# Expert slots: VectorE and ScalarE in written order, with the weight splits dealt out by a sequencer

## The chip, the cores and the metric

One Trainium2 chip, one core of it. The metric is the device time of one execution in microseconds (us), the median of three timed runs. One further execution was profiled; its trace is what is read here.

## What is computed

Causal attention (2 batches, 12 heads, 448 tokens, head size 64), then a dense layer with a squared rectifier, then a mixture of 8 experts in which every token goes to one expert:

```python
x = attention(q, k, v)                                # 896 tokens x 768
h = np.maximum(x @ w_in, 0.0); x = h * h @ w_out      # 768 -> 2048 -> 768
xn = x / (norm(x) + 1e-6); en = emb / (norm(emb) + 1e-6)
idx = argmax(xn @ en.T / tau); gate = softmax(xn @ en.T / tau)[idx]
for e in range(8):
    h = np.maximum(x[idx == e] @ w1[e], 0.0)          # 768 -> 1024
    out[idx == e] = gate * (h @ w2[e])                # 1024 -> 768
```

## The kernel before, in words

All products run in fp32r, each operand split into a high and a low part, and three products (high-high, high-low, low-high) are summed in PSUM. The first 377 us are attention, the dense layer (`phase_a`, `b_tiles`) and the routing of the first tiles; they are not touched. What follows is a row of expert slots, each with one expert's weights and a fixed number of tokens:

- **Slot E** (form D, 256 tokens of the expert that is fullest after five of seven tiles) starts at 377 us. While it runs, the generator `first()` finishes the routing of the last tile (`route_tile`: logits, norm, one-hot `OH`, ranks) and then the tables of all other slots (`tables`, then `table` with the product `tabp`, L600). It advances a step at each "hook": `ft0` lists the column blocks of the first product (`mm1_w`, eight blocks `ft`), `ft1` and `ft2` the row blocks of the second (`mm2`, eight blocks `fc`) for its two halves of 128 tokens. The hooks are built as a dictionary with the block's number as key. After the table come the gathers of the next slot's tokens (`slot_x`, L831, an indirect DMA from `ydram` issued by POOL) and their transposes `xt` on PE (L841).
- **Slots M0, T2, M1, T3, L0, T4** follow (the first is the rest of slot E's expert, the numbers are the table's). M has 160 tokens (128 and 32), T has 64, L has 384 (a D pass of 256 and an S pass of 128).

Each slot's weights are 16 tiles of 128x768. Eight DMAs by SP bring two tiles each into one of six raw buffers; ScalarE copies a tile into its high part `mh` (L59), VectorE subtracts it into the low part `ml` (L66). A tile takes the place of the same tile of the slot before, so it can be split only when PE has read that one for the last time, and the raw buffer comes free only when both its tiles are split.

The products are evicted by the same two engines. In M (`mm1_w`) ScalarE copies one half of the PSUM tile to `hsum` (L710), VectorE adds the other half (L711), ScalarE rectifies each part (L715) and VectorE forms the low parts (L716). In T and S (`mm1_x`) the same pair leaves `hr` (L777, L778), PE transposes it (`turn`, L751), and rectifier and low part follow (L753, L754). All these PSUM tiles, and the `xt` and `yt` ones, come from one pool, `ps_h`, of three buffers. Results leave as `osb` (L814 to L817).

PE's order is written by hand (`manual_schedule`). The order of VectorE and ScalarE is found by a list scheduler, which ranks ready instructions by its own estimates and so spreads the table work and the weight splits wherever an engine looks free.

Of the kernel before, what the change touches and what calls it, by code (L numbers as in the profile page):

```python
# [13 lines left out]
ALU = mybir.AluOpType  # L14
# [6 lines left out]
P = 128  # L21
# [11 lines left out]
def f32(ap):  # L33
    return ap.bitcast(F32)
# [5 lines left out]
    turn2=[1, 3], ft0=[0, 1, 2, 3, 4], ft1=[3], ft2=[2, 4, 5, 6], ew=[2, 4, 10, 10, 10, 12, 14], stop=0, mlo="V", xh="A", h2="A",  # L40
# [4 lines left out]
    vh="AG", kl="G", vl="G", pth="AAAA", nrm="GGGGGGG", u0=1, order=[2, 1, 3, 0, 4])  # L45


def build(tc, qkd, vd, w_in, w_out, emb, tau, wm, cst, out, dbg_y=None):
# [618 lines left out]
    def pieces(s, res):  # L667

        for i2 in range(8):
            if i2 == 0 or (i2 == CFG["first"] and s[4] is not None):  # L670
                ereg = nc.sync.value_load((s[3] if i2 == 0 else s[4])[0:1, :], min_val=0, max_val=E - 1)
            r = state["raw"] % (NXR + 2)
            state["raw"] += 1
            if r < NXR:
                raw = mo["xraw"][:, r]
            else:
                raw = spool.tile([P, 2 * DM], F32, tag="raw", name="mraw")
            DMA.dma_start(out=raw, in_=wm[bass.ds(ereg, 1), :, 2 * i2:2 * i2 + 2, :].rearrange("o p a c -> (o p) (a c)"))
# [9 lines left out]
            yield  # L688
# [5 lines left out]
    def mm1_w(s, w, hooks):  # L694
# [3 lines left out]
        for ft in range(8):  # L698
            step(hooks, ft)
            ps = ps_h.tile([P, 512], F32, tag="h", name="hps")  # L700
            if s[0] == "M":
# [26 lines left out]
            V.scalar_tensor_tensor(out=lo, in0=x, scalar=0.0, in1=f32(hi), op0=ALU.max, op1=ALU.subtract)  # L728

# [13 lines left out]
    def mm1_x(s, w, hooks):  # L743
# [13 lines left out]
        for q in range(4):  # L757
# [21 lines left out]
            hrs.append(hr)  # L779

# [91 lines left out]
    def mm1(s, w, hooks):  # L872
        return (mm1_w if s[0] in "DM" else mm1_x)(s, w, hooks)
# [37 lines left out]
    def tables():  # L911
# [18 lines left out]
        z = z.rearrange("p e k -> p (e k)")  # L930
        key = small([NZ], "key")
# [5 lines left out]
        V.reduce_sum(out=zr, in_=gt, axis=AX.X)  # L937
        zc = small([NZ, len(STEPS)], "zc")
# [12 lines left out]
        V.tensor_tensor(out=zo, in0=zo, in1=over, op=ALU.mult)  # L951
        zp = small([E, NK], "zp")
# [18 lines left out]

        k3 = small([NTI, NK], "k3")
# [14 lines left out]
        V.tensor_tensor(out=k3[:, :, 0:NK - 1], in0=k3[:, :, 0:NK - 1], in1=k3[:, :, 1:], op=ALU.subtract)  # L987
        tokw = bpool.tile([P, NTI, E, NK], BF16, tag="ysb", bufs=2, name="tokw")
# [30 lines left out]
    def run_slot(ps, w, feeds, at_end=False):  # L1019
# [8 lines left out]
        if len(ps) == 2:  # L1028
# [5 lines left out]
            more = mm1(ps[1], w, {})  # L1034
            it = feeds()
            if CFG["joint"]:
                next(it, None)
                mm2([(s, 1), (ps[1], 0)], w, hooks_for(CFG["xfj"], it, more))
            else:
                mm2([(s, 1)], w, more or {})  # L1040
                next(it, None)
                mm2([(ps[1], 0)], w, hooks_for(CFG["xfd"], it))
# [5 lines left out]
        parts = [(s, i) for i in range(len(FORM[s[0]]))]
        if len(parts) == 2 and not CFG["joint"]:
            mm2(parts[:1], w, hooks_for(CFG["xfd"], it, more))  # L1050
            all_of(it)
            mm2(parts[1:], w, {})
        else:
            mm2(parts, w, hooks_for(CFG["xfd"], it, more), split=at_end)
            all_of(it)
# [10 lines left out]

    it = first()
# [6 lines left out]
    all_of(it)  # L1074
    for i, ps in enumerate(slots_now):
        w = ew
        if i:
            w, it = slot_w(ps[0])
            all_of(it)
# [100 lines left out]
```

## Time and profile before

| | us |
|---|---|
| three timed runs | 584.53, 585.80, 588.54 (median 585.8) |
| profiled execution | 583.95 |
| its span, first to last instruction | 582.2 |
| PE busy in the span | 558.6 (96%) |
| VectorE (DVE) busy | 399.6 (69%) |
| ScalarE (ACT) busy | 291.5 (50%) |

An engine's busy time is the time in which at least one of its instructions is under way. PE's matmuls overlap one another, so PE counts as busy also where they follow at half pace. "Granted clock" is the share of TensorE's full clock of 2.4 GHz; 0.5 is the lower of its two levels, 1.2 GHz.

### The profile page before, as it was taken

How to read it: one execution, taken by the hardware profiler on the slowest of the kernel's cores; microseconds unless marked ns; L12 is line 12 of the kernel's file. 1: busy time of each engine (PE TensorE's matmuls, PEld its weight loads, DVE VectorE, ACT ScalarE, POOL GpSimd, SP SyncE). 2: the span in 40 equal slices, each digit the busy share in tenths (PEclk: the TensorE clock that was granted, in tenths of full speed). 3: DMA queues.
4: the chain of work that ended last, by engine and by line, in shares of the span. 5: the costliest groups of instructions: out<-in, count | busy, mean ns of one | idle time of the engine just before them, and what ended most of it. 6: DMA issues, size and time to landing. Idle time of an engine off the chain costs nothing.

```text
span 582.2 us, 9781 instructions
## 1 busy us (share of the span) xinstructions
PE 558.6 (96%) x3501; PEld 512.2 (88%) x3501; DVE 399.6 (69%) x901; ACT 291.5 (50%) x654; POOL 188.3 (32%) x204
## 2 busy tenths in 40 slices
PE   6999999999999999999999999899998999899994
PEld 3888788889999999999999999799997888799993
DVE  6878688955777878597664376975387986932641
ACT  4768678523343433434333226721478877923651
POOL 7676667854445544221000001001203412500010
PEclk8899999999999999999999999999999999899998
DMA  7757542223444655351000009404887987950310
GB/s 222 176 145 230 125 100 70 84 81 110 156 148 142 204 177 184 130 179 70 23 28 28 1 28 377 164 3 149 306 254 239 339 329 237 337 176 29 110 49 5
DMA packets 28233, 86.51 MB, mean 149 GB/s; under 512 B 2822, under 2 KB 13062, under 8 KB 28176
## 3 DMA queue, kind: packets, MB, share of 16 engines
q1 hardware_dynamic: 26640, 79.51, 42.3%
q0 software_dynamic: 1536, 6.29, 2.9%
q8 instruction: 29, 0.48, 0.3%
q14 instruction: 28, 0.23, 0.1%
HBM read 75.24 MB, written 6.29 MB: 140 GB/s over the span
## 4 chain that ended last, share of the span: by engine, by line
PE 85%; DVE 5%; DMA 4%; ACT 3%; issue 2%; SPq 1%; POOL 0%; POOLq 0%; ACTq 0%
PE yps L500 19%; PE ops L797 10%; PE pa L290 7%; PE pa L289 7%; PE pa L288 7%; PE pv L264 6%; PE s L215 5%; PE pt L247 3%; PE hps L707 3%; DMA q<-qs 3%; PE ops L739 3%; PE ops L734 2%; DVE ml L66 2%; PE hps L723 2%; PE hps L722 2%
## 5 line engine op out<-in xcount | busy, mean ns | idle before, releaser
L66 DVE TENSOR_TENSOR ml<-xraw,mh 128x768 fp32r<-128x768 f32 x64 | 60.1, 953 | 15.4 <-ACT mh L59 15.3
L59 ACT ACTIVATE mh<-xraw 128x768 fp32r<-128x768 f32 x64 | 53.3, 845 | 18.8 <-PE ops L734 9.3
L215 PE MATMUL s<-kh,q 128*128 128x128 f32 (+6 forms) x168 | 53.5, 352 | 4.3 <-ACT p L219 4.3
L797 PE MATMUL ops<-mh,act 128*128 128x384 f32 x224 | 53.5, 341 | 0.0
L819 POOL DMA_INDIRECT out<-osb,fsi x10 | 24.3, 2432 | 88.9 <-ACT osb L814 63.8
L230 POOL TENSOR_SCALAR p<-p,rs 128x192 f32<-128x192 f32 (+6 forms) x84 | 44.2, 545 | 17.9 <-ACT p L219 11.0
L264 PE MATMUL pv<-pt,v 128*128 128x448 f32 (+7 forms) x288 | 48.6, 303 | 0.2 <-DVE pt L66 0.2
L219 ACT ACTIVATE p<-s,mn 128x192 f32<-128x192 f32 (+6 forms) x84 | 39.5, 475 | 10.9 <-DVE mn L218 7.0
L123 DVE SCALAR_TENSOR_TENSOR w<-raw,w 128x768 int32<-128x768 int32 x32 | 42.8, 1339 | 0.7
L264 PEld LDWEIGHTS pv<-pt,v 128*128 128x128 f32 (+3 forms) x288 | 36.9, 163 | 5.4 <-issue 0.3
L215 PEld LDWEIGHTS s<-kh,q 128*128 128x128 f32 x168 | 35.5, 215 | 6.2 <-ACT p L219 4.9
L797 PEld LDWEIGHTS ops<-mh,act 128*128 128x128 f32 x224 | 39.2, 188 | 0.8
L66 DVE TENSOR_TENSOR ml<-mraw,mh 128x768 fp32r<-128x768 f32 x32 | 30.1, 953 | 14.3 <-ACT mh L59 14.3
L831 POOL DMA_INDIRECT xr<-ydram,fgi x10 | 10.7, 1067 | 89.3 <-DVE fsi L609 47.1
L66 DVE TENSOR_TENSOR hs<-h,hs 128x512 fp32r<-128x512 f32 (+1 forms) x32 | 21.9, 691 | 24.6 <-ACT hs L59 24.4
L218 DVE TENSOR_REDUCE mn<-s 128x1 f32<-128x192 f32 (+6 forms) x84 | 34.3, 415 | 5.7 <-PE s L216 5.5
L121 DVE SCALAR_TENSOR_TENSOR w<-raw,w 128x768 int32<-128x768 int32 x32 | 36.0, 1127 | 0.7
L294 ACT ACTIVATE relu<-pa 128x448 f32<-128x448 f32 x32 | 17.1, 537 | 36.3 <-PE pa L290 36.3
L119 DVE TENSOR_SCALAR w<-raw 128x768 int32<-128x768 int32 x32 | 22.2, 694 | 18.7 <-POOL wi3l L66 6.7
L66 DVE TENSOR_TENSOR pt<-pt 128x512 fp32r<-128x512 f32 x48 | 32.4, 680 | 3.1 <-ACT pt L59 3.1
L247 PE MATMUL pt<-ident,p 128*128 128x128 f32 x192 | 32.1, 284 | 0.0
L59 ACT ACTIVATE pt<-pt 128x512 fp32r<-128x512 f32 x48 | 28.1, 599 | 5.9 <-PE pt L247 3.8
(457 smaller groups left out, 1656.9 us busy)
## 6 DMA issues: line engine op xcount, KB each, us to landing
xraw<-in_wm SPq DMA_DIRECT2D x32, 768.0 KB, 6.3
raw<-in_w_in SPq DMA_DIRECT2D x16, 768.0 KB, 4.1
raw<-in_w_out SPq DMA_DIRECT2D x16, 768.0 KB, 4.2
mraw<-in_wm SPq DMA_DIRECT2D x16, 768.0 KB, 5.4
qk<-in_qkd SPq DMA_DIRECT2D x11, 448.0 KB, 4.8
q<-qs SPq DMA_DIRECT2D x22, 224.0 KB, 3.3
v<-in_vd SPq DMA_DIRECT2D x12, 256.0 KB
ydram<-ysb SPq DMA_DIRECT2D x7, 384.0 KB, 2.3
```

What stands on the lines that cost most here:

```text
L59: A.activation(out, in_, AF.Copy, scale=scale)
L66: eng.tensor_tensor(out=lo, in0=x, in1=hi, op=ALU.subtract)
L123: V.scalar_tensor_tensor(out=w[:, x], in0=raw[:, x, 0], scalar=29, in1=w[:, x], op0=ALU.logical_shift_right, op1=ALU.bitwise_or)
L215: T.matmul(ss, d["q2"][:, c, :, :, x].rearrange("p a b -> p (a b)"), d[y][:, :n], start=i == 0, stop=False)
L230: G.tensor_scalar(out=p, in0=p, scalar1=rs[:, COL[c]:COL[c] + 1], scalar2=1.0, op0=ALU.mult, op1=ALU.mult)
L247: T.transpose(pt[:, o * P:(o + 1) * P], d["p"][c][:, j * P:(j + 1) * P], ident)
L264: T.matmul(d["pv"][:, j * P:S] if h else d["pv"][0:D, j * P:S], d[x][0:k, j, 1:3].rearrange("p a b -> p (a b)") if h else d[x][0:k, j, 0], ...
L288: T.matmul(ps, wh[:, c], xhi[:, kc, gs], start=(kc == 0), stop=False)
L289: T.matmul(ps, wh[:, c], xlo[:, kc, gs], start=False, stop=False)
L290: T.matmul(ps, wl[:, c], xhi[:, kc, gs], start=False, stop=(kc == KC - 1))
L500: T.matmul(ps[t][c][:, :384], x, w[:, c * 384:(c + 1) * 384], start=(f == 0 and w is wh and x is hi), stop=(f == NF - 1 and x is lo))
L797: T.matmul(ps[c], x, ww[:, c * 384:(c + 1) * 384], start=(fc == 0 and x is hh and ww is wh), stop=(fc == 7 and x is hl))
```

## The change

VectorE and ScalarE now stand in the order of the source from slot E's first product on (`man2`), as PE did before. So that this order is a usable one, three things are written into it.

1. `tables()` gets five more yields, and the hooks `ft0=[0..7]`, `ft1=[0, 0, 3, 3]` (before: `[0..4]` and `[3]`). As the hooks are a dictionary, a block that is listed twice has one entry.
2. A sequencer feeds the weight splits. `freed(k)` notes that the written PE order has passed the last use of tile k; `pace(x)` adds x to a credit (at most 3) after a block and issues one tile's split (`feed_one`) for each whole unit of it, as far as tiles are free. The amounts are in `pc`: per block of the first and second product, D (1.4, 0.8), S (1.0, 1.0), M (1.0, 1.7), T (1.0, 0.4). A tile that is needed and not yet split is fed on demand (`Weights.__getitem__`).
3. In M the two parts' hidden values lie side by side (`mo["hm"]`), and one rectifier does both (8 fewer ScalarE instructions in each of two M slots).

```diff
-    turn2=[1, 3], ft0=[0, 1, 2, 3, 4], ft1=[3], ft2=[2, 4, 5, 6], ...
+    turn2=[1, 3], ft0=[0, 1, 2, 3, 4, 5, 6, 7], ft1=[0, 0, 3, 3], ft2=[2, 4, 5, 6], ...
+    pc=dict(D=(1.4, 0.8), S=(1.0, 1.0), M=(1.0, 1.7), T=(1.0, 0.4)))
...
+    def feed_one():
+        i = 1 + fd["done"] // 16
+        if fd["done"] % 16 == 0:
+            fd["it"] = pieces(fd["seq"][i][0], fd["w"][i])
+        next(fd["it"])
+        fd["done"] += 1
+
+    def pace(x):
+
+        if not fd["seq"]:
+            return
+        fd["credit"] = min(fd["credit"] + x, 3.0)
+        while fd["credit"] >= 1 and fd["done"] < min(fd["free"], 16 * (len(fd["seq"]) - 1)):
+            feed_one()
+            fd["credit"] -= 1
...
         for ft in range(8):
             step(hooks, ft)
+            if ft and ft % 2 == 0:
+                fin(ft - 2)
+                fin(ft - 1)
+            if ft:
+                pace(CFG["pc"][s[0]][0])
...
-                for part, m in enumerate(FORM["M"]):
-                    hi, lo = h_at(ft, part, m)
-                    x = hs[:, part * P:part * P + m]
-                    A.activation(hi, x, AF.Relu)
-                    V.scalar_tensor_tensor(out=lo, in0=x, scalar=0.0, in1=f32(hi), op0=ALU.max, op1=ALU.subtract)
+
+                hi = mo["hm"][:, ft, 0:n]
+                A.activation(hi, hs, AF.Relu)
+                for t0, t1, at in ((0, P, n + n - P), (P, n, n)):
+                    V.scalar_tensor_tensor(out=mo["hm"][:, ft, at:at + t1 - t0], in0=hs[:, t0:t1], scalar=0.0,
+                                           in1=f32(hi[:, t0:t1]), op0=ALU.max, op1=ALU.subtract)
...
             hrs.append(hr)
+            fin(2 * q)
+            fin(2 * q + 1)
+            pace(CFG["pc"][s[0]][0])
...
+                if cs[-1] == 1:
+                    fin(8 + fc)
+                    pace(CFG["pc"][parts[-1][0][0]][1])
...
+    man2 = tc.manual_schedule(engines={mybir.EngineType.DVE, mybir.EngineType.Activation})
+    man2.__enter__()
     it = first()
     for i, at in enumerate((CFG["ft0"], CFG["ft1"], CFG["ft2"])):
         hooks = {k: [it] for k in at}
```

What this makes of the engines' orders, at three places. First VectorE in slot E, around the norm of the last tile (`ynr`, `ynt`: a chain of small dependent steps from `ss` to `OH`; `yhl` and `lgs` belong to the logits; `act<-hps` is the eviction of one block of the slot's first product). Before:

```order
L452 TENSOR_SCALAR ynr<-ss 128x1
L454 TENSOR_SCALAR ynr<-ynr 128x1
L66 TENSOR_TENSOR yhl<-yt,yhl 128x3x128
L457 SCALAR_TENSOR_TENSOR ynt<-ynr,ss 128x1
L458 TENSOR_SCALAR ynt<-ynt 128x1
L459 TENSOR_TENSOR ynr<-ynr,ynt 128x1
L728 SCALAR_TENSOR_TENSOR act<-hps,act 128x2x128
L457 SCALAR_TENSOR_TENSOR ynt<-ynr,ss 128x1
L66 TENSOR_TENSOR yhl<-yt,yhl 128x3x128
```

The chain starts ahead of block 0's eviction. VectorE in the same place now:

```order
L67 TENSOR_TENSOR yhl<-yt,yhl 128x3x128
L780 SCALAR_TENSOR_TENSOR act<-hps,act 128x2x128
L67 TENSOR_TENSOR yhl<-yt,yhl 128x3x128
L780 SCALAR_TENSOR_TENSOR act<-hps,act 128x2x128
L537 COPY lgs<-lgt 16x256
L780 SCALAR_TENSOR_TENSOR act<-hps,act 128x2x128
L453 TENSOR_SCALAR ynr<-ss 128x1
L455 TENSOR_SCALAR ynr<-ynr 128x1
L458 SCALAR_TENSOR_TENSOR ynt<-ynr,ss 128x1
```

The whole chain now stands behind the evictions of blocks 0, 1 and 2; 22 steps of it end with `OH`, which PE's `rk` needs behind block 3.

PE in slot E's second product (`ops`; six of its 128x384 rows are one block `fc`), from the table's product `tabp` on. Before:

```order
L797 MATMUL ops<-ml,act 128x384 x2
L797 MATMUL ops<-mh,act 128x384 x2
L600 MATMUL tabp<-rv,ol 128x108 x7
L797 MATMUL ops<-mh,act 128x384 x2
L797 MATMUL ops<-ml,act 128x384 x2
L797 MATMUL ops<-mh,act 128x384 x4
L797 MATMUL ops<-ml,act 128x384 x2
```

There it stands ahead of the first half's block 3, and seven whole blocks lie between it and the first `xt`. PE now, from `tabp` to that `xt`:

```order
L855 MATMUL ops<-mh,act 128x384 x2
L602 MATMUL tabp<-rv,ol 128x108 x7
L855 MATMUL ops<-mh,act 128x384 x2
L855 MATMUL ops<-ml,act 128x384 x2
L855 MATMUL ops<-mh,act 128x384 x4
L855 MATMUL ops<-ml,act 128x384 x2
L855 MATMUL ops<-mh,act 128x384 x2
L903 MATMUL xt<-ident,xr 128x128 x3
```

`tabp` has moved to the second half's block 2 and `xt` has stayed, so two blocks lie between.

ScalarE where slot M0 ends and T2 begins (`osb` is M0's result, `hr` the eviction of T2's first product, `mh` the high parts of weight tiles). Before:

```order
L845 CAST act<-xt 128x6x64
L59 ACTIVATE mh<-xraw 128x768 x4
L814 ACTIVATE osb<-ops,fgate 128x384 x2
L816 ACTIVATE osb<-ops,gate_4669 32x384 x2
L59 ACTIVATE mh<-xraw 128x768
L59 ACTIVATE mh<-mraw 128x768
L777 COPY hr<-hps 64x256
```

Now:

```order
L907 CAST act<-xt 128x6x64
L60 ACTIVATE mh<-xraw 128x768 x5
L876 ACTIVATE osb<-ops,fgate 128x384 x2
L878 ACTIVATE osb<-ops,gate_4721 32x384 x2
L831 COPY hr<-hps 64x256
L60 ACTIVATE mh<-mraw 128x768 x2
L831 COPY hr<-hps 64x256
```

The last tile of T2 has gone ahead of `osb`, and the first two of M1 behind the first `hr`.

## Rows read from the trace of the kernel before

**Rows 1.** The page's part 1: busy time, share of the span, instructions.

```profile
PE 558.6 (96%) x3501; PEld 512.2 (88%) x3501; DVE 399.6 (69%) x901; ACT 291.5 (50%) x654; POOL 188.3 (32%) x204
```

**Rows 2.** Busy time by stage: E's first product, T2, M1, T3.

```profile
core 0: us, PE busy (x) PEld busy (x) DVE busy (x) ACT busy (x) POOL busy (x), PEclk, DMA share, GB/s
377.00:396.00 19.00, 18.39 (x156) 17.80 (x155) 15.75 (x82) 5.16 (x14) 0.00 (x0) 1.00 0.06 23
...
442.00:461.00 19.00, 17.19 (x107) 14.03 (x107) 17.87 (x29) 17.79 (x32) 9.91 (x4) 0.91 0.87 305
461.00:489.00 28.00, 26.97 (x181) 24.81 (x182) 21.62 (x45) 19.57 (x45) 4.51 (x2) 1.00 0.86 296
489.00:507.00 18.00, 15.78 (x100) 13.26 (x99) 16.67 (x27) 16.54 (x31) 9.11 (x4) 0.91 0.87 303
```

**Rows 3.** The longest of PE's waits, 340 to 583 us: total, times, longest.

```profile
PE hps L734 <- DVE hr L778: 2.7, 2, 1.4
```

**Rows 4.** Busy time by stage, as rows 2: just behind the waits of T2 and T3.

```profile
450.00:454.00 4.00, 3.95 (x19) 2.83 (x18) 4.00 (x9) 3.43 (x7) 4.00 (x1) 0.57 0.82 273
...
498.00:501.50 3.50, 3.50 (x14) 2.53 (x15) 3.50 (x7) 2.56 (x6) 2.65 (x1) 0.51 0.95 299
```

**Rows 5.** Timeline of PE in slot E: start, us, instruction, idle before and releaser.

```profile
387.19 0.18 PE L560 MATMUL rk<-OH,tri 128*128 128x8 bf16 x1
...
387.65 0.17 PE L913 MATMUL cnt<-OHs,ones 128*128 128x8 bf16 x1 [0.26 <-DVE c L572]
```

**Rows 6.** Timeline of VectorE (DVE) in slot E.

```profile
381.27 0.15 DVE L458 TENSOR_SCALAR ynt<-ynt 128x1 f32<-128x1 f32 x1
381.45 0.16 DVE L459 TENSOR_TENSOR ynr<-ynr,ynt 128x1 f32<-128x1 f32 x1
...
385.43 0.42 DVE L728 SCALAR_TENSOR_TENSOR act<-hps,act 128x256 fp32r<-128x256 f32 x1
...
386.64 0.22 DVE L557 TENSOR_SCALAR OH<-ct,m 128x8 bf16<-128x8 f32 x1
```

**Rows 7.** Timelines of PE and POOL, one chain piece (a block), and all gathers' landing.

```profile
399.88 0.99 PE L600 MATMUL tabp<-rv,ol 128*128 128x108 f32 x7 [0.35 <-DVE ol L597]
...
402.14 1.00 POOL L831 DMA_INDIRECT xr<-ydram,fgi  x1 [47.07 <-DVE fsi L609]
...
408.07 0.49 PE L841 MATMUL xt<-ident,xr 128*128 128x128 f32 x3
...
410.98 1.06 PE ops L797 x6
...
DMA to landing us min/median/max: 4.8/7.7/8.8
```

**Rows 8.** Timelines of PE and DVE in M0: its two products' starts, an add, a split.

```profile
415.70 0.31 PE L707 MATMUL hps<-act,mh 128*128 128x320 f32 x1
...
428.10 0.55 PE L797 MATMUL ops<-mh,act 128*128 128x384 f32 x2
...
417.73 0.33 DVE L711 TENSOR_TENSOR hsum<-hps,hsum 128x160 f32<-128x160 f32 x1 [4.46 <-ACT hsum L710]
418.99 0.96 DVE L66 TENSOR_TENSOR ml<-xraw,mh 128x768 fp32r<-128x768 f32 x1 [0.94 <-ACT mh L59]
```

**Rows 9.** Timelines of PE and ACT in T2: start, results, a split, evictions, block 3.

```profile
442.87 0.28 PE L734 MATMUL hps<-mh,act 128*128 128x256 f32 x1
...
443.27 1.04 ACT L816 ACTIVATE osb<-ops,gate 32x384 f32<-32x384 f32 x2
444.34 0.85 ACT L59 ACTIVATE mh<-xraw 128x768 fp32r<-128x768 f32 x1
...
445.94 0.37 ACT L777 COPY hr<-hps 64x256 f32<-64x256 f32 x1
...
449.55 0.28 ACT L753 ACTIVATE act<-ht 128x128 fp32r<-128x128 f32 x1
...
449.49 0.38 PE L734 MATMUL hps<-mh,act 128*128 128x256 f32 x1 [1.35 <-DVE hr L778]
```

More of the change, by code (lines that the diff above doesn't have):

```diff
@@ L39 @@
     joint=1, mhi="A", rt6=[1, 4, 7, 9, 15], woh="A", h2h="A", h2l="V", rt=[1, 3, 5, 7, 10], et=[9, 10, 14],
-    turn2=[1, 3], ft0=[0, 1, 2, 3, 4], ft1=[3], ft2=[2, 4, 5, 6], ew=[2, 4, 10, 10, 10, 12, 14], stop=0, mlo="V", xh="A", h2="A",
+    turn2=[1, 3], ft0=[0, 1, 2, 3, 4, 5, 6, 7], ft1=[0, 0, 3, 3], ft2=[2, 4, 5, 6], ew=[2, 4, 10, 10, 10, 12, 14], stop=0, mlo="V", xh="A", h2="A",
     wh="G", wil="G", wol="GV", warm=6, nsa=6, nwi=3, nwb=3, wo0=4, hs0=[4, 5, 8, 9], conv0=17, convs=2, pin=1,
@@ L493, in b_tiles @@
                         es.enter_context(tc.issue_after(last["oh"].ins))
-                    next(hooks[-1], None)
+                    for _ in range(2):
+                        next(hooks[-1], None)
             wh, wl = wo[f]
@@ L657, in alloc_moe @@
         mo["h"] = act[:, 3072:7168].rearrange("p (f b t) -> p f b t", f=8, b=2)
+        n = sum(FORM["M"])
+        mo["hm"] = act[:, 3072:7168].rearrange("p (f c) -> p f c", f=8)[:, :, 0:2 * n]
     def h_at(fs, part, n, m=1):
@@ L687, in pieces, with fed, freed, __init__ @@
                 res.append((hi, lo))
-            yield
+                yield
+    fd = dict(seq=[], now=0, done=0, free=0, credit=0.0, it=None)
+    def fed(i, k=0):
+        return 16 * (i - 1) + k
+    def feed_one():
[11 more added lines that the diff above has]
+            fd["credit"] -= 1
+    def freed(k):
+        if fd["seq"]:
+            fd["free"] = max(fd["free"], 16 * fd["now"] + k + 1)
+    class Weights(list):
+        def __init__(self, i):
+            self.i = i
+        def __getitem__(self, k):
+            while len(self) <= k:
+                feed_one()
+            return list.__getitem__(self, k)
+    nop = lambda k: None
     FORM = dict(D=(P, P), M=(P, 32), S=(P,), T=(64,))
-    def mm1_w(s, w, hooks):
+    def mm1_w(s, w, hooks, fin=nop):
         xh, xl = mo["xh"], mo["xl"]
@@ L741, in two_pass, with mm1_x @@
             high()
-    def mm1_x(s, w, hooks):
+    def mm1_x(s, w, hooks, fin=nop):
         xh, xl = mo["xh"], mo["xl"]
@@ L779, in mm1_x, with mm2 @@
             hrs.append(hr)
+            fin(2 * q)
+            fin(2 * q + 1)
+            pace(CFG["pc"][s[0]][0])
         rest = iter([lambda: turn(2, hrs[2]), lambda: turn(3, hrs[3])])
         return {t: [(f() for f in rest)] for t in CFG["turn2"]}
-    def mm2(parts, w, hooks, split=False):
+    def mm2(parts, w, hooks, split=False, fin=nop):
         pss = [[ps_y.tile([P, 512], F32, tag=f"y{c}", name="ops")[:, :384] for c in range(2)] for _ in parts]
@@ L793, in mm2 @@
                     if FORM[s[0]][part] == P:
-                        hh, hl = h_at(fc, part, P)
+                        hh, hl = h_at(fc, part, P) if s[0] != "M" else (
+                            mo["hm"][:, fc, 0:P], mo["hm"][:, fc, -P:])
                         for x, ww in ((hh, wh), (hh, wl), (hl, wh)):
@@ L800, in mm2 @@
                         m = FORM[s[0]][part]
-                        two_pass([ps[c] for c in cs], mo["h"][:, fc, part, 0:2 * m],
-                                 *([x[:, c * 384:(c + 1) * 384] for c in cs] for x in (wh, wl)), fc, 8, m)
+                        x = mo["hm"][:, fc, P:P + 2 * m] if s[0] == "M" else mo["h"][:, fc, part, 0:2 * m]
+                        two_pass([ps[c] for c in cs], x,
+                                 *([ww[:, c * 384:(c + 1) * 384] for c in cs] for ww in (wh, wl)), fc, 8, m)
+                if cs[-1] == 1:
+                    fin(8 + fc)
+                    pace(CFG["pc"][parts[-1][0][0]][1])
         for (s, part), ps in zip(parts, pss):
@@ L870, in all_of, with mm1 @@
             pass
-    def mm1(s, w, hooks):
-        return (mm1_w if s[0] in "DM" else mm1_x)(s, w, hooks)
+    def mm1(s, w, hooks, fin=nop):
+        return (mm1_w if s[0] in "DM" else mm1_x)(s, w, hooks, fin)
     man = tc.manual_schedule(engines={mybir.EngineType.PE})
@@ L970, in tables @@
         ear.update(ei=ei, fi=fi)
+        yield
         k3 = small([NTI, NK], "k3")
@@ L1033, in run_slot @@
             all_of(it)
-            more = mm1(ps[1], w, {})
+            more = mm1(ps[1], w, {}, freed)
             it = feeds()
[L1036 to L1042, printed above, removed]
+            next(it, None)
+            mm2([(s, 1), (ps[1], 0)], w, hooks_for(CFG["xfj"], it, more), fin=freed)
             all_of(it)
             return
-        more = mm1(s, w, {})
+        more = mm1(s, w, {}, freed)
         it = feeds()
         next(it, None)
[L1048 to L1055, printed above, removed]
+        mm2([(s, i) for i in range(len(FORM[s[0]]))], w, hooks_for(CFG["xfd"], it, more), split=at_end, fin=freed)
+        all_of(it)
     slots_now = None
@@ L1074, in build @@
     all_of(it)
+    fd.update(seq=slots_now, w=[ew] + [Weights(i) for i in range(1, len(slots_now))])
     for i, ps in enumerate(slots_now):
[L1076 to L1079, printed above, removed]
+        w = fd["w"][i]
+        fd["now"] = i
         def feeds():
@@ L1085, in build @@
         run_slot(ps, w, feeds, i == NSS)
+    fd["seq"] = []
+    man2.__exit__(None, None, None)
     man.__exit__(None, None, None)
```

8 lines of the change are left out of this document (7 added, 1 removed).

## The prediction

> **What bounds the kernel now.** I read the page's busy times first. PE is busy for 96% of the span [rows 1], so whatever the change does to VectorE and ScalarE counts only where PE waits for them. Next I read the busy times by stage, to find the stages with idle PE time and lowered clock. Slot E's first product has 0.6 us of idle time in 19; T2 has 1.8 in 19, M1 1.0 in 28, T3 2.2 in 18, and T2 and T3 show a mean clock of 0.91 [rows 2]. In T2 and T3 VectorE and ScalarE are busy all but 1.1 to 1.5 us: there the two splitting engines, not PE, set the pace. The view of PE's waits names the eviction of T's first product, `hr`, as the largest part [rows 3]. Last, the stages cut finer: behind T2's waits the clock is 0.57 over 4 us, behind T3's 0.51 over 3.5 us, where E and M1 have 1.00 [rows 2, 4]. At half clock 3.4 us of work cost 1.7 us more, so each T slot loses about 2 us by waits and 1.7 by clock. That is all the change can win: some 8 us in T2, M1 and T3. Everything ahead of 377 us stays as it is.
>
> **The change part by part.** The sum is made against the profiled execution, 583.95 us.
>
> *The routing chain in slot E.* PE's `rk` needs `OH`. Before, the norm steps ran ahead of the logits, between the first evictions, and `OH` came at 386.64, half a microsecond before PE wanted it at 387.19 [rows 5, 6]. Now all 22 steps stand behind the eviction of block 2, which began at 385.43 and took 0.42 [rows 6]; it had a table step ahead of it, so I let it begin at 385.2 and end at 385.6. A dependent step follows its forerunner by 0.18 us [rows 6]; with 0.19 for a mean, 22 steps take 4.2 us, so `OH` is there at 389.8 and PE waits 2.6 us. Then `cnt` needs `OHs`, which stands behind block 3's eviction; that one's rectifier stands on ScalarE behind the softmax's exponential, itself inside the chain. I put `cnt` at 390.55 against 387.65 [rows 5]: **+2.9 us**. Bounds: +2.0, with a step at 0.15, the shortest one's own time, and +3.5, with 0.22, the own time of `OH` [rows 6]. The later table steps cost nothing here: no PE instruction between `cnt` and `tabp` waits for them, and block 7's eviction, which they push back by some 3 us, is wanted only in the last block of the second product, 7 us after its start.
>
> *The table and the gather.* This is the largest term. Before, the gather was issued 2.26 us after `tabp` began (402.14 - 399.88), and `xt` ran at 408.07 without waiting, so the data had landed within 5.9 us [rows 7]. PE had seven blocks of 1.05 us in between. Now it has `tabp` itself and two blocks, 0.85 + 2.1 = 2.95 us. The landing is between 4.8 us, the fastest gather of this trace, and the 5.9 of this very gather. `xt` can start 7.1 to 8.2 us after `tabp`, and PE waits 4.1 to 5.2 us; I take the middle, **+4.7 us**. With the median landing of 7.7 it is 7.0. SP's weight loads for T2, five of which also hang on the table, move by as much and meet the gather as they did before. The wait of 0.35 us at `tabp` [rows 7] goes, as `rv` and `ol` are now ready long before: **-0.35**.
> The Trainium skill, "DMA: Bandwidth & Descriptors", section "Anatomy of one DMA — SWDGE (gpsimd) path", fits the time of one such DMA as about 2.0 us plus its bytes over 436 thousand per us. For 128 rows of 3 KB that would be 2.9 us, the wait would shrink to 2.2, and the sum would be 2.5 us lower. Of the twelve gathers in this trace none landed in under 4.8 us [rows 7], so it gets no chance here.
>
> *M0's first product.* PE needs 12.4 us for eight blocks, 1.55 each [rows 8]. In strict order ScalarE and VectorE do two blocks and then two splits, and each link waits for the other engine: add 0.33, rectifier 0.28, twice; then one `mh` of 0.85, and two `ml` of 0.96, the second hidden for a tenth in the first's end [rows 8, 9]. With hand-overs the circle is 4.4 us for two blocks that take PE 3.1. The first circle's add ends at 2.4 us after M0's start, the fifth block's add at 11.6. PE wants that buffer of the three for block 7 at 10.9: **+0.8 us** (bounds 0 and 2, since before, the same work in a looser order cost nothing here).
>
> *T2.* M0's last tile, 0.85 us, and its two pairs of `osb`, 1.05 each, stand ahead of T2's first `hr` on ScalarE [rows 9]. So `hr` starts at T2's start + 2.95, against 445.94 - 442.87 = 3.07 before [rows 9]. Two splits still stand behind each of the first two `hr`, so VectorE's second add ends at about +6.35, and block 3, which wants that buffer, starts at +6.4 against 6.62 [rows 9]. The win comes later, where one split now stands between evictions instead of two: about 0.6 us of small waits. **-0.8 us** in all; bounds 0 and -1.8, all the idle time that there is [rows 2].
>
> *M1 and T3.* M1 has one split per block: add, rectifier, `mh`, `ml` make 2.4 us against PE's 1.55, and with two spare buffers block 7 waits about 1.1 us, as much as M1 idles now [rows 2]: **0**. At M1's end ScalarE has 13 tiles behind the last rectifier and runs some 2.5 us late into `osb`; T3's block 3 then starts no earlier than before, and only the later small waits go: **-0.5 us** (bounds +1 and -2.2).
>
> *One rectifier in M.* 16 ScalarE instructions go, on an engine that waits for VectorE's adds in M; 0, with -0.5 as a bound. L0, T4 and the end have PE work enough to cover the splits: 0.
>
> *The clock.* The two low stretches followed some 2 us of waits within about 5 us. T2's and T3's stay, since their waits do. Slot E's two new waits, 2.9 and 4.7 us, are as long or longer. Nothing here shows how long a wait must be, so I count one more stretch for the two: **+1.7 us** (bounds 0 and 3.4).
>
> Sum: 2.9 + 4.7 - 0.35 + 0.8 - 0.8 + 0 - 0.5 + 1.7 = +8.45 us, that is 592.4 for an execution like the profiled one. The median before lies 1.85 us above that execution, so the forecast for the median is **594.2 us**.
>
> **The rivals.**
>
> *The splits stop delaying the T slots (not slower).* The mechanism is the place of `hr` ahead of the splits on ScalarE and VectorE. If block 3 finds its buffer in time, the waits of T2 and T3 go, 1.8 + 2.2 us, and with them both low stretches, 3.4. That is 7.4 us instead of my 1.3, and 588.1 with the rest of my sum; without a low stretch in slot E, 586.4, no change. It decides once block 3 of T2 starts before +5 us. For it: the two engines' total work per slot does fit. Against it: `osb` and two splits still stand ahead of the second `hr`.
>
> *The gather lands late, and the clock falls twice in slot E (slower still).* With the median landing, 7.7 us, the wait is 7.0 instead of 4.7; two stretches instead of one add 1.7: 594.2 + 2.3 + 1.7 = 598.2. For it: the weight loads fall into the same moment. Against it: they did so before, and this gather was in time.
>
> *The hooks do what the list says.* `ft1` names blocks 0 and 3 twice. With four steps `tabp` would stay ahead of block 3 and the gather term would fall away with its clock term: 594.2 - 4.7 - 1.7 = 587.8. The order of PE speaks against it: `tabp` stands at the second half's block 2. No chance of its own.
>
> **How the numbers follow.** A measurement of this kernel can tell about 1%, 5.9 us, from no change. The forecast with its bounds, 590 to 597, has 0.55; the late gather 0.18; the relieved T slots 0.22; a win elsewhere, with slot E costing next to nothing, 0.05. Slower by over 1% (above 591.7) are the late gather and all but 0.03 of the forecast: 0.70. Faster by over 1% (below 579.9) are the win elsewhere and 0.01 of the relieved slots: 0.06. The remaining 0.03 and 0.21 are within 1%: 0.24. The range reaches from the relieved T slots without a further low stretch, 586.4, to the late gather with M0 and T3 at their upper bounds, about 600.
>
> **What would show it.** In the profile of the changed kernel: PE waits of 2 to 3 us at `rk` for `OH`, and of 4 to 5 us at the first `xt` with a gather as releaser; M0's first product starts 7 to 9 us later than at 415.70, and the stretch from there to L0 is about as long as before; a clock near 0.5 for 3.4 us around the gather's wait. The forecast is wrong if `xt` does not wait, if T2 or T3 keep a clock of 1.00, or if M0 waits by several us.

## The result, and the profile after

The changed kernel takes 593.92 us (median; 590.41 to 594.74) against 586.43 for the kernel before, timed beside it: ratio 1.0116, 95% interval 1.0075 to 1.0157. The forecast was 594.2, slower. Its profiled execution took 594.67, 10.7 over the one of before, with a span of 592.9. The page's part 1 answers to [rows 1]:

```profile
PE 561.0 (95%) x3501; PEld 515.6 (87%) x3501; DVE 405.0 (68%) x901; ACT 288.4 (49%) x638; POOL 174.9 (30%) x204
```

PE has little more to do and more to wait for. Its waits from 340 us on, which answer to [rows 3]:

```profile
PE xt L903 <- DMA xr<-ydram,fgi: 5.5, 1, 5.5
PE rk L562 <- DVE OH L559: 2.7, 1, 2.7
PE hps L788 <- DVE hr L832: 2.2, 2, 1.7
PE xt L903 <- DVE act L67: 2.1, 1, 2.1
PE cnt L975 <- DVE c L574: 1.2, 1, 1.2
PE hps L758 <- DVE hsum L762: 0.9, 2, 0.5
PE ht L805 <- DVE hr L832: 0.8, 1, 0.8
```

`xt`, `rk` and `cnt` at the top are new and all three lie in slot E. To see what they cost, the span is cut at the start of each slot's work on PE: E's first product, E's second, M0, T2, M1, T3, L0. The columns are those of [rows 2]; the length less PE's busy time is PE's idle time, and a longer busy time at a lower clock is the clock's share. Before:

```profile
377.02:396.24 19.22, 18.61 (x159) 18.02 (x158) 15.97 (x84) 5.14 (x14) 0.00 (x0) 1.00 0.06 23
396.24:415.70 19.46, 19.11 (x118) 18.35 (x116) 5.95 (x20) 2.71 (x6) 4.97 (x5) 1.00 0.77 274
415.70:442.87 27.17, 27.17 (x184) 25.13 (x183) 18.53 (x40) 18.90 (x44) 1.95 (x2) 1.00 0.73 229
442.87:460.83 17.96, 16.15 (x102) 13.20 (x101) 17.02 (x29) 16.79 (x30) 9.91 (x4) 0.90 0.87 313
460.83:489.32 28.49, 27.46 (x182) 25.26 (x183) 22.11 (x45) 20.06 (x46) 4.51 (x2) 1.00 0.85 293
489.32:507.65 18.33, 16.11 (x101) 13.60 (x101) 17.00 (x28) 16.87 (x31) 9.76 (x4) 0.91 0.88 309
507.65:560.96 53.31, 53.28 (x381) 52.45 (x381) 24.69 (x37) 23.79 (x42) 3.04 (x3) 1.00 0.29 98
```

After:

```profile
378.28:402.52 24.24, 20.25 (x158) 19.50 (x157) 15.22 (x67) 5.03 (x14) 0.00 (x0) 0.93 0.05 18
402.52:429.46 26.94, 21.48 (x117) 20.62 (x116) 9.83 (x37) 2.71 (x6) 4.99 (x5) 0.87 0.61 216
429.46:457.26 27.80, 27.39 (x183) 25.17 (x183) 19.06 (x40) 17.17 (x34) 2.15 (x2) 1.00 0.61 195
457.26:474.89 17.63, 15.92 (x102) 13.49 (x101) 14.10 (x24) 13.30 (x25) 4.51 (x4) 0.90 0.81 272
474.89:503.03 28.14, 27.60 (x183) 25.21 (x183) 21.40 (x45) 19.50 (x38) 1.98 (x2) 1.00 0.68 223
503.03:518.86 15.83, 14.57 (x101) 12.69 (x101) 14.72 (x26) 12.94 (x26) 5.28 (x4) 1.00 0.99 385
518.86:571.55 52.69, 52.69 (x382) 52.32 (x381) 31.95 (x45) 29.58 (x51) 1.95 (x2) 1.00 0.47 153
```

Slot E is 12.5 us longer: 5.0 in the first product (3.4 of idle time, 1.6 of clock) and 7.5 in the second (5.1 and 2.4). The slots behind it are 3.2 us shorter, 2.5 of them in T3, whose clock is now 1.00. The two low stretches of slot E, which answer to [rows 4]:

```profile
392.70:396.10 3.40, 3.40 (x18) 3.40 (x18) 0.96 (x7) 0.00 (x0) 0.00 (x0) 0.51 0.00 0
...
420.00:427.00 7.00, 5.58 (x22) 5.08 (x22) 1.11 (x2) 0.96 (x2) 0.98 (x1) 0.51 1.02 387
```

Both are at the lower of the clock's two levels. Another 1.3 us lie ahead of 377 us, where nothing was changed; they belong to this execution.

The timeline of PE in slot E after, which answers to [rows 5] and [rows 7]:

```profile
391.05 0.18 PE L562 MATMUL rk<-OH,tri 128*128 128x8 bf16 x1 [2.68 <-DVE OH L559]
...
392.44 0.17 PE L975 MATMUL cnt<-OHs,ones 128*128 128x8 bf16 x1 [1.19 <-DVE c L574]
...
412.93 0.88 PE L602 MATMUL tabp<-rv,ol 128*128 128x108 f32 x7
...
421.42 0.87 PE L903 MATMUL xt<-ident,xr 128*128 128x128 f32 x3 [5.46 <-DMA xr<-ydram,fgi]
```

And VectorE there, which answers to [rows 6] (the eviction of block 2, the chain's first step and its last):

```profile
386.27 0.42 DVE L780 SCALAR_TENSOR_TENSOR act<-hps,act 128x256 fp32r<-128x256 f32 x1 [1.72 <-ACT act L779]
386.61 0.14 DVE L453 TENSOR_SCALAR ynr<-ss 128x1 int32<-128x1 int32 x1
...
390.76 0.23 DVE L559 TENSOR_SCALAR OH<-ct,m 128x8 bf16<-128x8 f32 x1
...
392.23 0.16 DVE L574 TENSOR_TENSOR c<-rk,OH 128x8 f32<-128x8 f32 x1
```

The chain of 22 steps runs from 386.61 to the end of `OH` at 390.99, and PE's `rk` follows at once. `cnt` does not wait for `OHs`, which was there at 391.61; it waits for `c`, the step that reads `rk`, as the two share one PSUM buffer (`ps_r`). Ahead of `c` stand block 3's eviction, `OHs` and five small steps for the gate. POOL issues the first gather at 415.11, 2.18 us after `tabp` began, and `xt` follows 6.31 us after that issue; it could have started at 415.96, after two blocks.

### The profile page after: what moved, and what is told of

It reads as the page before. It is cut to its first block, busy times and chain, and to the rows that moved or that the text cites. A ratio compares the mean times of both kernels' runs of the same rounds, so it can differ in the third digit from the quotient of the medians.

```text
span 592.9 us, 9725 instructions
## 1 busy us (share of the span) xinstructions
PE 561.0 (95%) x3501; PEld 515.6 (87%) x3501; DVE 405.0 (68%) x901; ACT 288.4 (49%) x638; POOL 174.9 (30%) x204
## 4 chain that ended last, share of the span: by engine, by line
PE 64%; DVE 16%; DMA 8%; ACT 4%; issue 4%; POOL 1%; SPq 1%; POOLq 0%; DVEq 0%; ACTq 0%
PE yps L502 15%; PE ops L855 10%; PE pv L265 6%; PE s L216 5%; DVE w L122 3%; DVE w L124 3%; PE pt L248 3%; DVE ml L67 3%; PE ops L793 3%; PE ops L788 2%; PE pa L290 2%; PE pa L291 2%; PE pa L289 2%; DMA q<-qs 2%; DVE w L120 2%
## 5 line engine op out<-in xcount | busy, mean ns | idle before, releaser
L855 PE MATMUL ops<-mh,act 128*128 128x384 f32 x224 | 54.9, 348 | 0.0
L881 POOL DMA_INDIRECT out<-osb,fsi x10 | 11.0, 1098 | 98.3 <-ACT osb L876 67.6
L60 ACT ACTIVATE pt<-pt 128x512 fp32r<-128x512 f32 x48 | 28.1, 599 | 6.3 <-PE pt L248 4.3
L855 PE MATMUL ops<-ml,act 128*128 128x384 f32 x112 | 29.3, 343 | 0.0
```

The source lines that it names most:

```text
L60: A.activation(out, in_, AF.Copy, scale=scale)
L855: T.matmul(ps[c], x, ww[:, c * 384:(c + 1) * 384], start=(fc == 0 and x is hh and ww is wh), stop=(fc == 7 and x is hl))
```

## The experiments

Lengths in us, cut as above; the ratio is to the kernel before, timed in the same job. It is an estimate over the timed runs and differs from the quotient of the two medians by up to 0.3%.

| run | ratio (95% interval) | E first | E second | M0 | T2 | M1 | T3 | L0 |
|---|---|---|---|---|---|---|---|---|
| before | | 19.2 | 19.5 | 27.2 | 18.0 | 28.5 | 18.3 | 53.3 |
| changed | 1.0116 (1.0075-1.0157) | 24.2 | 26.9 | 27.8 | 17.6 | 28.1 | 15.8 | 52.7 |
| tab_early | 1.0154 (1.0113-1.0194) | 24.0 | 26.4 | 27.8 | 19.3 | 28.1 | 15.9 | 52.7 |
| norm_early | 1.0112 (1.0059-1.0164) | 20.7 | 25.6 | 27.8 | 16.7 | 28.1 | 15.8 | 52.7 |
| both_early | 1.0113 (1.0061-1.0164) | 20.7 | 26.5 | 27.8 | 19.3 | 28.1 | 15.9 | 52.8 |
| before_tab_late | 1.0117 (1.0078-1.0156) | 18.7 | 26.3 | 27.2 | 18.1 | 28.5 | 17.9 | 53.3 |
| slots_only | 0.9914 (0.9880-0.9947) | 19.2 | 19.7 | 27.8 | 18.3 | 28.1 | 15.8 | 52.7 |
| rectifier_only | 0.9988 (0.9958-1.0017) | 19.2 | 20.1 | 27.2 | 18.0 | 28.5 | 17.8 | 53.4 |
| interleaved_E | 0.9982 (0.9954-1.0010) | 20.5 | 20.3 | 27.8 | 17.6 | 28.1 | 15.8 | 52.7 |
| slots_scheduler | 0.9993 (0.9965-1.0022) | 18.7 | 19.6 | 27.2 | 19.4 | 28.5 | 19.1 | 53.3 |
| no_carry | 0.9929 (0.9905-0.9953) | 19.3 | 19.7 | 27.8 | 15.3 | 28.1 | 15.9 | 54.2 |
| M0_scheduler | 0.9929 (0.9906-0.9953) | 19.2 | 19.7 | 27.8 | 17.6 | 28.1 | 15.9 | 52.7 |
| M0_scheduler_no_carry | 0.9933 (0.9907-0.9958) | 18.7 | 19.6 | 27.8 | 15.3 | 28.1 | 15.9 | 54.2 |
| T2_zero_credit | 0.9855 (0.9827-0.9883) | 19.2 | 19.8 | 27.2 | 14.8 | 28.1 | 15.8 | 52.7 |

**The place of the table.** First two kernels that move `tabp` alone, one in either direction. In the kernel before, the hook that puts it early is taken out:

```diff
-    ft1=[3]
+    ft1=[]
```

> The kernel before with one thing moved: no hook in the second product's first half, so that the table's product, the gather and the transposes stand on PE where the changed kernel has them; VectorE and ScalarE stay with the list scheduler. Theory A, the distance of gather and transposes alone makes the cost: a wait of 4.5 to 5.6 us at the first xt, half clock behind it, +6 to +8 us, ratio 1.011 to 1.014. Theory B, it costs only where VectorE is in strict order and the table comes late: the wait is under 1 us, ratio 1.00.

Its longest wait of PE:

```profile
PE xt L841 <- DMA xr<-ydram,fgi: 5.5, 1, 5.5
```

Theory A: the late table alone makes the second product 6.9 us longer, 5.2 of idle time and 1.7 of a clock of 0.50 for 6.8 us that sets in during the wait, and the ratio is that of the whole change. The other direction, in the changed kernel:

```diff
-    ft1=[0, 0, 3, 3]
+    ft1=[0, 1, 3]
```

> The changed kernel with the table's product and the gather back ahead of the first half's block 3 (second-product hooks at 0, 1 and 3 instead of 0 and 3); nothing else differs. Theory A, the gather is too near its transposes: the wait of 5.5 us at the first xt goes, and with it the 6.8 us at half clock behind it, of which about 5.5 us were PE work and cost 2.7. M0's first product then starts about 8 us earlier than in the changed kernel; the waits at rk and cnt (2.7 and 1.2 us) stay. Ratio to the kernel before about 0.998 (585 us). Theory B, the strict order of VectorE costs time all along and the gather's wait only takes it up: the wait turns up elsewhere in slot E, ratio at least 1.008 (591 us).

```profile
PE tabp L602 <- DVE ol L599: 4.3, 1, 4.3
```

Theory B. The gather's wait is gone, and 4.3 us of wait for `ol` stand in its place: in written order VectorE isn't done with the table's operands when PE reaches the early place. The hooks put `tabp` late, but VectorE would have been late anyway.

**The norm chain.** The scale's 15 steps go directly behind the last half of the tile's `y`, ahead of the evictions; then this with the early table.

```diff
+            if c == 1 and t == NTI - 1:
+                sc = scale_of(ss)
...
-        nrm = norm_of(rpool, ss, P, "yn")
...
+        if t < NTI - 1:
+            sc = scale_of(ss)
```

> The changed kernel with the 15 norm steps of the last tile written behind its second yhl, ahead of block 1's eviction, so that seven steps instead of 22 lie between block 2's eviction and OH. Theory A: OH comes some 2.8 us earlier, rk waits under 0.3 us, cnt at most 1, and the half-clock stretch behind them, 1.7 us, goes: about 5 us, ratio to the kernel before 1.003 (588 us); the gather's wait of 5.5 us stays. Theory B, block 0 to 2's evictions are what is late: rk still waits over 1.5 us, ratio at least 1.009.

> Both edits in one: hooks at 0, 1, 3 and the norm steps early. Theory A, slot E carries the whole loss and the rest of the program is some 3 us shorter than before (M0 +0.6, T2 -0.3, M1 -0.4, T3 -2.5, L0 -0.6): no wait over 0.6 us at rk, cnt, tabp or xt in slot E, ratio to the kernel before 0.993 to 0.996 (582.5 to 584 us). Theory B, the order of the slots loses too and T3's gain was this one execution's: ratio 1.00 or more.

The longest waits in slot E of the first kernel, and the longest of the second, where `cnt` also waits 1.7:

```profile
PE xt L910 <- DMA xr<-ydram,fgi: 5.3, 1, 5.3
...
PE cnt L982 <- DVE c L581: 1.7, 1, 1.7
```

```profile
PE tabp L609 <- DVE ol L606: 4.3, 1, 4.3
```

`rk`'s wait is gone and the first product is 3.5 us shorter, so the chain's place is its cause, as theory A has it. The rest of A missed: `cnt` still waits 1.7 where at most 1 was expected, and the ratio is 1.0112, not 1.003. By the stages slot E is 4.9 us shorter than in the changed kernel, 0.8%; the ratio's interval, 1.006 to 1.016, can neither show nor exclude that, with timed runs from 587.43 to 592.61. Both repairs together missed A as well (0.993 to 0.996; measured 1.0113): slot E isn't back. But theory B, that the order of the slots loses too, isn't the reason either: the slots behind slot E are together 1.5 us shorter than before, and the loss lies in slot E, in `cnt`, `tabp` and a low stretch of the clock.

**The order inside the tables.** What is left is the way from `cnt` to `tabp` on VectorE: 16.2 us in both_early (406.32 - 390.14), 12.2 before (399.88 - 387.65). The next kernel writes the tables' two independent chains turn about, besides the early norm and the hook of before. Two steps for `fi` (about 0.45 us), which the table doesn't need, go behind it, and `OHs` goes ahead of the eviction that follows.

```diff
-    ft1=[0, 1, 3]
+    ft1=[3]
...
         V.scalar_tensor_tensor(out=key, in0=z, scalar=32.0, in1=c_zi, op0=ALU.mult, op1=ALU.add)
+        off = small([NTI], "off")
+        V.scalar_tensor_tensor(out=off, in0=k3[:, :, 1], scalar=-float(CAP), in1=ranks, op0=ALU.mult, op1=ALU.add)
+        V.tensor_tensor(out=again, in0=again, in1=k3[:, :, 0], op=ALU.subtract)
         gt = bpool.tile([P, NZ, NZ], BF16, tag="ysb", bufs=2, name="gt")
...
```

> The changed kernel with slot E's own order written out better: the fifteen steps of the last tile's norm right behind the halves of its y, the sum OHs ahead of the eviction that follows, the two independent chains of the tables (capacities; offsets and lanes) written turn about instead of one behind the other, one table step fewer and the hook of before (ft1 3), so that the matmuls of tabp and the gather stand where before has them. Slots as in the changed kernel. Theory A (dependent small steps in a row cost 0.17 us each and independent ones less, so turn about takes some 3 us out of the 16 from cnt to tabp): tabp waits under 1 us, E 19.5 to 20.7, E mm2 19.5 to 21, ratio 0.996 (0.993 to 1.000). Theory B (the number of steps sets the time, not their dependence): tabp waits 3 to 4.5 us for ol at its early place, as in the kernel with the early table, E mm2 24 to 26, ratio 1.006 to 1.011.

The way is 13.1 us now (404.62 - 391.51). VectorE's timeline: two steps of the offsets, of which the second needs the first (both_early), and a step of each chain side by side (interleaved_E).

```profile
401.50 0.17 DVE L1052 TENSOR_TENSOR again<-again,k 128x7 f32<-128x7 f32 x1
401.70 0.17 DVE L1053 SCALAR_TENSOR_TENSOR off<-again,off 128x7 f32<-128x7 f32 x1
```

```profile
394.74 0.17 DVE L1010 SCALAR_TENSOR_TENSOR key<-z,ct 128x16 f32<-128x16 f32 x1
394.82 0.16 DVE L1012 SCALAR_TENSOR_TENSOR off<-k,ranks 128x7 f32<-128x7 f32 x1
```

From start to start, here, it is 0.20 us where a step needs its forerunner and 0.08 where it does not, though each takes 0.17. VectorE's idle time at evictions is alike in both kernels on this way (2.1 and 1.9 us). Theory A then: of the 3.1 us saved 0.45 are the two steps moved and 0.2 less idle time, so about 2.4 are the turn-about order. PE's waits in slot E:

```profile
PE cnt L985 <- DVE c L584: 1.7, 1, 1.7
PE tabp L612 <- DVE ol L609: 1.2, 1, 1.2
```

`tabp` waits 1.2, a little over what A expected. `cnt`'s wait is as long as in the two kernels before, although `OHs` had been moved ahead: it hangs on `c`, ahead of which block 3's eviction and five steps for the gate stand. With all that slot E is 2.1 us longer than before, the slots gain 3.2, and the ratio is near 1.

**The slots alone.** Now slot E is left to the scheduler, with the hooks of before and without the five added yields, and the order of the source begins at M0.

```diff
-    man2 = tc.manual_schedule(engines={mybir.EngineType.DVE, mybir.EngineType.Activation})
-    man2.__enter__()
     it = first()
...
     all_of(it)
+    man2 = tc.manual_schedule(engines={mybir.EngineType.DVE, mybir.EngineType.Activation})
+    man2.__enter__()
     fd.update(seq=slots_now, w=[ew] + [Weights(i) for i in range(1, len(slots_now))])
```

> The changed kernel, but the order of the source holds for VectorE and ScalarE only from slot M0 on; in slot E the scheduler orders them, with the hooks of before (ft0 0 to 4, ft1 3) and without the four added steps in the tables. Sequencer, paces and the joint rectifier stay in the slots. Theory A (slot E carries the whole loss, the slots behind it gain): E as before, 19.2 and 19.5 us, the first tile transposes of M0 without a wait for the gather, M0 27.8, T2 17.6, M1 28.2, T3 15.8, L0 52.7, in sum 3.1 us under before: ratio 0.995 (0.991 to 0.998). Theory B (T3's 2.5 us are only where the low-clock stretches fell in the changed kernel, since E was shifted): T3 back at 18.3 with a half-clock stretch in it, ratio 1.000 (0.998 to 1.003). Theory C (the order of the source costs in the slots too, and the loss isn't E's alone): ratio over 1.003.

Theory A: 581.5 us against 585.63, faster than before by a little more than A's 0.995. So slot E held the whole loss. Which part of the slots' change does it, the next two kernels tell: the same without the order of the source (no `man2`), and the kernel before with the joint rectifier alone (the hidden layer's 160 columns in one piece, one activation).

> As the kernel with the change in the slots only, but VectorE and ScalarE are ordered by the scheduler in the slots as well: the sequencer still decides where each weight split is written, and the joint rectifier stays. Theory A (the engines' order is what gains in T3: the split no longer stands ahead of hr): T3 back at 18.3 with a half-clock stretch, sum of the slots as before, ratio 1.000 (0.997 to 1.003). Theory B (the sequencer's places are enough, whoever orders the engines): T3 at 15.8, ratio 0.995.

> The kernel before with one edit: in the M slots the hidden layer is kept in one piece of 160 columns and ScalarE rectifies it in one activation where it took two (128 and 32 columns). The scheduler's order elsewhere. Theory A (the record's term 0: ScalarE isn't waited for in M0 and M1): ratio 1.000 (0.998 to 1.002), M0 27.0 to 27.2, M1 28.3 to 28.6. Theory B (each evicted block comes 0.2 us sooner and the weight splits behind it too): 0.5 us in each M slot, ratio 0.998, and part of M1's gain in the changed kernel is the rectifier's.

T3 under the scheduler, cut as above (slots_scheduler):

```profile
494.32:513.44 19.12, 17.39 (x101) 14.83 (x101) 17.10 (x28) 16.96 (x31) 9.72 (x4) 0.82 0.91 309
```

Theory A in both. With the sequencer's places but the scheduler's order T3 is as long as before, with its low clock; every slot has the length of before, T2 and T3 up to 1.4 us more. The rectifier moves nothing: M0 27.2 and M1 28.5. So the gain needs the written order of the two engines; the sequencer under the scheduler gains nothing. Whether the written order would gain without the sequencer, no run shows.

What the written order changes can be counted. VectorE's weight splits alone (`ml`), in T3 and L0, before and changed (us, busy PE, PEld and VectorE, PEclk, DMA share, GB/s):

```profile
489.32:507.65 18.33, 10.86 (x40) 5.46 (x40) 13.08 (x15) 0.91 0.88 309
507.65:560.96 53.31, 32.41 (x120) 22.25 (x120) 16.95 (x18) 1.00 0.29 98
```

```profile
503.03:518.86 15.83, 10.04 (x40) 5.15 (x40) 10.18 (x12) 1.00 0.99 385
518.86:571.55 52.69, 32.40 (x120) 22.24 (x120) 24.21 (x27) 1.00 0.47 153
```

T3 has 12 splits where it had 15, T2 11 for 16, and L0, where PE doesn't idle, 27 for 18. In slots_scheduler the counts are those of before. In written order, then, the two short slots put off a part of the splitting that filled their engines.

The low clock is hardly part of T3's gain. In the scheduler's order T3 takes 17.85 us at full clock (before_tab_late) against 18.33 with a low stretch, and T2 17.96 at full clock (rectifier_only), as long as with a low stretch in before:

```profile
497.00:514.85 17.85, 14.93 (x102) 12.56 (x101) 16.91 (x28) 17.00 (x31) 10.56 (x4) 1.00 0.88 307
```

```profile
444.88:462.84 17.96, 14.94 (x101) 12.19 (x100) 17.02 (x29) 16.78 (x30) 11.53 (x4) 1.00 0.88 309
```

What PE's busy time lost there, its idle time gained. So at most 0.5 of the 2.5 us is the clock's.

**One split or two.** Why did T3 gain and T2 not? VectorE in the changed kernel at T2's first evictions:

```profile
460.94 0.40 DVE L832 TENSOR_TENSOR hr<-hps,hr 64x256 f32<-64x256 f32 x1
461.60 1.83 DVE L67 TENSOR_TENSOR ml<-mraw,mh 128x768 fp32r<-128x768 f32 x2 [0.27 <-ACT mh L60]
463.35 0.41 DVE L832 TENSOR_TENSOR hr<-hps,hr 64x256 f32<-64x256 f32 x1
```

And at T3's:

```profile
507.54 0.40 DVE L832 TENSOR_TENSOR hr<-hps,hr 64x256 f32<-64x256 f32 x1
507.87 0.94 DVE L67 TENSOR_TENSOR ml<-xraw,mh 128x768 fp32r<-128x768 f32 x1
508.74 0.41 DVE L832 TENSOR_TENSOR hr<-hps,hr 64x256 f32<-64x256 f32 x1
```

Two splits stand between the first two `hr` in T2, one in T3: the second `hr` starts 2.41 us after the first there and 1.20 here. T2 pays in two what M0 has left on the sequencer's account. So the credit was set to zero at each slot's start:

```diff
-        fd["now"] = i
+        fd["now"], fd["credit"] = i, 0.0
```

> The kernel with the change in the slots only, and one edit: the sequencer's credit is set to zero at the start of each slot, so that in T2 one weight split stands between two evictions of a hidden block where two stood (T3 has one already). Theory A (T3 lost its low-clock stretch and 2.5 us because one split instead of two stands ahead of the next hr, so that the longest wait for hr falls from 1.7 to 0.5 us): T2 falls from 18.3 to 15.8 to 16.0 us with the wait at 0.5 and no half-clock stretch in it; the other slots stay; ratio to before 0.987 (0.984 to 0.991). Theory B (T3 is short for another reason, what its own predecessor leaves behind it): T2 stays at 17.6 to 18.3, ratio 0.991 as without the edit.

T2 falls from 18.3 to 15.3 without a low stretch: theory A for T2, with a longest wait of 0.8 where 0.5 was expected. A part of the 3 us is clock: the order with two splits took 16.7 at full clock (norm_early), so the edit by itself gives 1.4. And it does two things, since T2 now also has 9 splits where it had 11; no run separates their number from their place. The other slots didn't stay, as A had it: L0 is 1.5 us longer, 1.0 of it busy time at full clock and 0.5 a wait that slots_only hasn't:

```profile
PE hps L776 <- DVE ml L67: 0.5, 1, 0.5
```

That it starts without what was saved up for its splits is the explanation that the last kernel puts to the test. The ratio, forecast at 0.987, is 0.9929 and can't be told from that of slots_only. The two kernels meant to leave M0 to the scheduler moved no row of VectorE or ScalarE, so they only repeat slots_only and no_carry; on M0 they say nothing:

```diff
-    man2.__enter__()
...
+        if i == 1:
+            man2.__enter__()
```

> The kernel with the change in the slots only, but the order of the source begins at T2: M0 is left to the scheduler too. Theory A (M0's 0.6 us come from the order of the source, in which an eviction's last half waits behind ScalarE's work): M0 27.2 us where it had 27.8, the rest as there, ratio 0.990 (0.987 to 0.993). Theory B (they come from where the sequencer puts the splits): M0 stays at 27.8, ratio 0.991. With M0's splits ordered by the scheduler T2's start may be packed as before: then T2 18.0 with a half-clock stretch.

> Both edits: M0 left to the scheduler, and the credit set to zero at the start of each slot. Theory A for both: M0 27.2, T2 15.8, T3 15.8, in sum 3 us under the kernel with the change in the slots only: ratio to before 0.986 (0.983 to 0.989). If M0's order by the scheduler leaves splits behind that stand ahead of T2's first evictions, T2 stays near 18 and the ratio near 0.990.

In the last kernel the order begins at T2 in fact, and the credit is zeroed there alone.

```diff
+        if i == 1:
+            fd["credit"] = 0.0
+            man2 = tc.manual_schedule(engines={mybir.EngineType.DVE, mybir.EngineType.Activation})
+            man2.__enter__()
```

> The kernel with the change in the slots only, and two edits that are read in different slots: the order of the source begins at T2 (here, other than in the run named M0_scheduler, M0's rows do move), and the credit is set to zero at T2's start alone, so that T2 has one split between evictions but L0 keeps what is saved up for it. Theory A (M0's 0.6 us are the order's; T2's 2.3 to 2.9 us are the single split's; the 1.5 us that L0 lost with the credit zeroed at every slot were that L0 had no saved splits at its start): M0 27.2, T2 15.3 to 16, M1 28.1, T3 15.8, L0 52.7, ratio 0.988 (0.985 to 0.991). Theory B (what T2 doesn't split is only paid for later, in L0): L0 at 54.2 again, ratio 0.991 to 0.993.

PE's one longer wait in T2, at block 3, and T2 cut as above:

```profile
449.41 0.39 PE L788 MATMUL hps<-mh,act 128*128 128x256 f32 x1 [0.26 <-DVE hr L832]
```

```profile
444.30:459.10 14.80, 14.54 (x103) 12.47 (x102) 12.24 (x22) 11.42 (x22) 4.53 (x4) 1.00 0.76 250
```

Theory A throughout: M0 27.2, T2 14.8 (15.3 to 16 expected) with 0.3 us of idle time and a full clock, L0 52.7. L0 has 29 splits here as in no_carry, so its 1.5 us there were not their number. The median is 578.28 us against 586.07, ratio 0.9855: faster than both kernels, and more than A's 0.988.

## Why the prediction was right, and where not

The sign, the places and the total were right: `rk` and `xt` wait, for `OH` and for the gather. That the total came out so close, 593.92 for 594.2, is luck: two errors of opposite sign made up for each other. Slot E cost 12.5 us where the sum had 8.95 (2.9 + 4.7 - 0.35 + 1.7), and the slots gained 3.2 where it had 0.5. The difference itself is not known that well: 10.7 between the profiled executions, 7.5 between the medians, with 8.45 forecast.

- *The chain.* `rk` waits 2.68 against 2.6 forecast, and norm_early shows that the chain's place does it. `cnt`'s shift is 3.5 (14.16 us after E's start against 10.63), the upper bound, not 2.9. The step that failed is "then `cnt` needs `OHs`": it needs `c` to have read `rk`, and the written order puts the eviction and five gate steps ahead of `c`. The line of `cnt` in [rows 5] had named `c` already.
- *The gather.* 5.46 against 4.7. The issue came as forecast (2.18 behind `tabp`; 2.26 assumed); the landing was 6.3 where 4.8 to 5.9 had been taken; why it came later is open. before_tab_late shows 5.5 by this cause alone. The Trainium skill's fit in "DMA: Bandwidth & Descriptors", section "Anatomy of one DMA — SWDGE (gpsimd) path", gave 2.9 us for the landing and a wait of 2.2; the trace does not agree.
- *The clock.* One stretch, 1.7, bounds 0 to 3.4: there were two, of 3.4 us behind the waits at `rk` and `cnt` and of 6.8 from within the gather's wait on, and PE's busy time in slot E grew by 1.64 + 2.37 = 4.0 us, beyond the upper bound. In T2 and T3 the premise failed that a low stretch costs 1.7: there it cost 0 and 0.5, as VectorE and ScalarE set the pace.
- *M0.* +0.6 against +0.8; with M0 under the scheduler it is 27.2 again, so it is the order's, as forecast. The size was partly chance: 2.4 plus two circles of 4.4 is 11.2, not 11.6, and the wait at block 7 by that 0.3. The trace has 0.41 there, the rest of the 0.6 is busy time.
- *T2.* -0.3 against -0.8. The second `hr` ended 6.50 us after T2's start, where +6.35 was forecast: two splits ahead of it.
- *M1, L0, the rectifier.* -0.35 and -0.6 against 0, and 0 against 0.
- *T3.* The step that failed is "only the later small waits go". Block 3 started 6.17 us after T3's start against 6.62, so 0.45 of the 2.5 us lie ahead of it and 2.05 behind. The sum kept T3's splits at their number; 12 were left of 15. Its longest wait fell from 1.4 to 0.8. The rival of the relieved T slots came true in this one place, without the early block 3 that it named and without its price for the clock; no_carry and T2_zero_credit bring T2 there too, with block 3 at 5.7 and 5.1 us.
- *The rival on the hooks* was priced wrongly. An earlier table saves nothing in this order, as `ol` is then what PE waits for (tab_early).

That the forecast would fail "if T2 or T3 keep a clock of 1.00" came true for T3; the forecast of the time stood only since slot E lost as much more.

## What to carry to other kernels

Put two engines in written order where each step's place is known and the work repeats, and leave a long chain of small steps to a scheduler that can fill it, or write the independent chains turn about yourself. Where two engines set the pace of a short stretch, look how much of their work a longer one, in which PE doesn't idle, can take over, and count what stands between two evictions on the same engine: one split instead of two there, and two fewer in the slot, were worth 1.4 us at full clock. When a repair doesn't show, look for the wait that took the old one's place before dropping the cause.

## What was not expected of the hardware

- A small VectorE step that needs the one before it starts 0.20 us after it, an independent one 0.08, with the same 0.17 us shown for each. The Trainium skill, "Vector Engine (DVE) Microarchitecture Reference", section "5.2 Measured stream behaviour on trn2 (trn3 not measured)", states about 75 ns per instruction after queue overlap plus 1.04 ns per column; for 7 columns that is an estimate of 0.08 us, which agrees with the independent steps. The dependent ones are more than twice that.
- The same order of T2 took 16.7 us in one profiled execution (norm_early), 17.6 in another (changed) and 19.3 in two (tab_early, both_early). The low clock behind its 1.7 us wait lasted 0, 3.4 and 6.8 us. A wait that is short by itself was so followed by up to 2.5 us more. In the scheduler's order, where VectorE and ScalarE set the pace, T2 took 17.96 us both with a stretch of 3.4 us and without. The timed runs of the changed kernel scatter from 590.41 to 594.74; how much of that is the clock, no run here shows.
